# Alternating the order of the two row tiles from one matmul pair to the next

## Chip, cores and metric

The kernel runs on one core of one Trainium2 chip. The metric is the device time of that core in microseconds (us), the median of several executions. Ratios are computed as the mean time of one kernel's fast runs over the mean time of the other's fast runs of the same rounds, so they are not quite the ratio of the medians quoted beside them; a 95% interval stands with each. A single run of a kernel is marked as such.

## The reference

A causal convolution over time with 7 taps per head (weights by softmax), then a two-layer network with a Swish whose slope is learned:

```python
# x [8, 4096, 192], weight [8, 7], w_in [192, 2048], w_out [2048, 192], beta [2048]
w = softmax(weight, axis=-1)
conv[b, s, head, :] = sum_k w[head, k] * x_padded[b, s + k, head, :]   # 6 zeros of padding in front
t = conv.reshape(32768, 192)
h = t @ w_in
g = h * sigmoid(beta * h)
out = g @ w_out                                                       # [32768, 192] float32
```

The two matrix products are nearly all the arithmetic.

## The kernel before

The 192 channels are three groups of 64, and batches are handled in two halves (`h`). Rows 0-63 of SBUF hold one half, rows 64-127 the other. (SBUF tiles are what the matmuls read; PSUM tiles are what they write; TensorE does the matmuls, ScalarE the Swish, named `Silu` in the code, VectorE sums and copies.) So a matmul with a contraction of 64 uses only half of the rows of the array, and two of them, one on rows 0-63 (**tile A** below) and one on rows 64-127 (**tile B**), stream at the same time: the records below show them start 19 ns apart and go on for 82 or 216 ns. A *pair* is one matmul on each tile. The hidden layer uses the tiles for the two halves of the batch; the output layer uses them for the two halves of a 128-row contraction, whose partial sums VectorE adds afterwards. The two matmuls of a pair write different slices (`[:, 0]` and `[:, 1]`) of a PSUM tile.

```python
def hidden(s, fc):                     # one block of 128 hidden features, 2 x 512 tokens
    ...
    for j in range(NG):                # NG = 3 channel groups
        for h in range(2):
            rows = slice(h * DG, (h + 1) * DG)                    # 0-63, 64-127
            nc.tensor.matmul(ph[:, h, 0:n], w_in_s[rows, j, cols], cts[s][rows, j, 0:n],
                             start=(j == 0), stop=(j == NG - 1))  # 512 columns
    nc.scalar.activation(gs[s][:, fc, :, 0:n], ph[:, :, 0:n], AF.Silu, scale=beta[:, fc:fc+1])

def output(s, u):                      # 8 pairs: half of the 16 feature blocks of 128 tokens
    ...
    for i in range(u * per, (u + 1) * per):
        blk, fc = divmod(i, NF)
        ...
        for r in range(2):
            rows = slice(r * 64, (r + 1) * 64)
            nc.tensor.matmul(po[:, r, b * D : (b + 1) * D],
                             g[rows, fc, h, q * BLK : (q + 1) * BLK], w_out_s[rows, fc, :],
                             start=(fc == 0), stop=(fc == NF - 1))  # 192 columns
        ...                            # after fc 15: VectorE copies, adds, and a DMA stores

for s in range(N_ST + 1):              # N_ST = 33 steps, and a last pass with outputs alone
    for u in range(NF):                # 16 units a step
        if s < N_ST: hidden(s, u)
        if s > 0:    output(s - 1, u)
        ...                            # VectorE taps of a later convolution, DMA
```

A *period* is one unit: 3 hidden pairs and 8 output pairs, 22 matmuls. Each matmul has its own weight load, the instruction that puts its stationary operand into the array.

Of the kernel before, what the change touches and what calls it, by code (L numbers as in the profile page):

```python
# [17 lines left out]
def kernel(  # L18
# [335 lines left out]
    def hidden(s, fc):  # L354
        n = steps[s][2]
        if fc == 0:
            gs[s] = g_pool.tile([128, NF, 2, TOK], BF16, name="g")
        ph = psum_h.tile([128, 2, TOK], FP32, name="ph")
        cols = slice(fc * 128, (fc + 1) * 128)
        for j in range(NG):  # L360
            for h in range(2):
                rows = slice(h * DG, (h + 1) * DG)
                nc.tensor.matmul(  # L363
                    ph[:, h, 0:n],
                    w_in_s[rows, j, cols],
                    cts[s][rows, j, 0:n],
                    start=(j == 0),
                    stop=(j == NG - 1),
                )
        nc.scalar.activation(  # L370
            gs[s][:, fc, :, 0:n], ph[:, :, 0:n], AF.Silu, scale=beta[:, fc : fc + 1]
        )
# [3 lines left out]
    def store(s, h, q, n_q, osb):  # L376

        ch, t0, n = steps[s]
        p, c = divmod(ch, CHUNKS)
        if s < N_ST - 1:  # L380
            if q < n // BLK - 1:
                return
            n_q = n // BLK
        t = c * TOK + t0 + (q + 1 - n_q) * BLK
        nc.sync.dma_start(
            out=out_v[h, p, t : t + n_q * BLK, :].rearrange("(b q) d -> q b d", q=BLK),
            in_=osb[:, q + 1 - n_q : q + 1, :],
        )

    def output(s, u):  # L390

        g = gs[s]
        nb = steps[s][2] // BLK
        per = 2 * nb
        for i in range(u * per, (u + 1) * per):
            blk, fc = divmod(i, NF)
            h, q = divmod(blk, nb)
            b = q % 2

            single = s == N_ST - 1 and h == 1 and q >= nb - 2  # L400
            if single:
                b = 0
            if fc == 0 and b == 0:
                state["po"] = psum_o.tile([128, 2, TOK], FP32, name="po")
            if fc == 0 and q == 0:
                state["osb"] = osb_pool.tile([128, TOK // BLK, D], FP32, name="osb")
            po, osb = state["po"], state["osb"]
            for r in range(2):
                rows = slice(r * 64, (r + 1) * 64)
                nc.tensor.matmul(  # L410
                    po[:, r, b * D : (b + 1) * D],
                    g[rows, fc, h, q * BLK : (q + 1) * BLK],
                    w_out_s[rows, fc, :],
                    start=(fc == 0),
                    stop=(fc == NF - 1),
                )
            if fc == NF - 1 and (b == 1 or single):
                n_q = 1 if single else 2
                cols = slice((b + 1 - n_q) * D, (b + 1) * D)
                dst = osb[:, q + 1 - n_q : q + 1, :].rearrange("p b d -> p (b d)")  # L420
                if single:
                    nc.scalar.copy(dst, po[:, 0, cols])  # L422
                else:
                    nc.vector.tensor_copy(dst, po[:, 0, cols])  # L424
                nc.vector.tensor_tensor(dst, po[:, 1, cols], dst, ALU.add)  # L425
                store(s, h, q, n_q, osb)
# [19 lines left out]
    for s in range(N_ST + 1):  # L446
        if s + 2 < N_ST:
            queue.extend(conv_ops(s + 2))
        for u in range(NF):
            if s < N_ST:  # L450
                hidden(s, u)
            if s > 0:
                output(s - 1, u)
            if s == 0 and u in first_work:
                first_work[u]()
            n = pops.get(s, 24)
            pops_u = (u + 1) * n // NF - u * n // NF if s else u > 5
            for _ in range(pops_u):
                if queue:
                    queue.popleft()()  # L460
            if u == 0 and s + 4 < N_CH:
                cast(s + 4)
            if u == 1 and s + 2 < N_CH:
                xpose(s + 2)
# [30 lines left out]
```

## Time and profile before

| | before |
|---|---|
| time, median (first 3 runs) | 697.0 us (696.14 to 697.85) |
| TensorE busy in the profile | 99% |
| granted TensorE clock | 1.00 |
| one period in the steady part | 1.307 us |

From the page of the kernel before: busy time by engine (first line), and the chain of work that ended last, by engine and by line of the program (line 363 is the hidden matmul, line 410 the output matmul). PE is TensorE's matmuls, PEld its weight loads, DVE is VectorE, ACT is ScalarE, POOL is GpSimd. The granted clock is the share of its full speed that TensorE was allowed.

```profile
PE 686.9 (99%) x11465; PEld 525.9 (76%) x11465; DVE 553.2 (80%) x935; ACT 578.7 (83%) x545; POOL 69.8 (10%) x83
...
PE 96%; DVE 3%; ACT 0%; issue 0%
PE po L410 48%; PE ph L363 46%; DVE ct L346 2%; DVE ct L344 1%; PE ph L204 1%; PE ph L249 0%; PE po L236 0%; PE po L208 0%; DVE w_in_s L149 0%; ACT g L370 0%; PE po L249 0%; DVE xt L314 0%; DVE osb L425 0%; DVE ct L300 0%; DVE osb L424 0%
```

The costliest groups of the same page: count, busy time, mean duration of one, idle time before them and what ended it.

```profile
L370 ACT ACTIVATE g<-ph,beta 128x1024 bf16<-128x1024 f32 (+1 forms) x528 | 571.8, 1088 | 97.0 <-PE ph L363 93.1
L410 PEld LDWEIGHTS <-g 64*128 64x128 bf16 x8192 | 368.9, 94 | 102.4 <-issue 0.2
L410 PE MATMUL po<-w_out_s,g 64*128 64x192 bf16 x8192 | 429.8, 243 | 0.0
L363 PE MATMUL ph<-ct,w_in_s 64*128 64x512 bf16 (+1 forms) x3168 | 425.5, 370 | 2.8 <-ACT g L370 1.4
```

TensorE is the bound: it waits for ScalarE 1.4 us in all, while ScalarE waits for it 93.1 us. In the timeline of TensorE in the middle of the run (start, duration, engine, line, operation, count) one sees the period.

```profile
299.63 0.83 PE L363 MATMUL ph<-ct,w_in_s 64*128 64x512 bf16 x6
300.28 0.84 PE L410 MATMUL po<-w_out_s,g 64*128 64x192 bf16 x16
300.94 0.83 PE L363 MATMUL ph<-ct,w_in_s 64*128 64x512 bf16 x6
301.59 0.66 PE L410 MATMUL po<-w_out_s,g 64*128 64x192 bf16 x11
```

From 299.63 to 300.94 is one period. The durations of the two rows overlap: a record lasts 376 ns (512 columns) or 243 ns (192), but the same tile starts its next matmul 216 or 82 ns after the start. The ends of matmuls are modelled in this profile; the distance between starts is what counts. Single records of the trace give it (listed from the trace, times in us; `waits` and `signals` mark the matmul that waits for ScalarE to free PSUM and the one that tells ScalarE that the group is done):

```
before   start     after the one before it
output   201.486   63 ns
output   201.506   20 ns
hidden   201.569   63 ns     waits
hidden   201.588   19 ns
hidden   201.785  197 ns
hidden   201.804   19 ns
hidden   202.001  197 ns
hidden   202.020   19 ns     signals
```

Two starts 19 ns apart are one pair. The same tile starts again 63 + 19 = 82 ns later (192 columns; 82.4 on average) or 197 + 19 = 216 ns later (512 columns): 3 x 216 + 8 x 82.4 = 1307 ns, the whole period.

### The profile page before, as it was taken

How to read it: one execution, taken by the hardware profiler on the slowest of the kernel's cores; microseconds unless marked ns; L12 is line 12 of the kernel's file. 1: busy time of each engine (PE TensorE's matmuls, PEld its weight loads, DVE VectorE, ACT ScalarE, POOL GpSimd, SP SyncE). 2: the span in 40 equal slices, each digit the busy share in tenths (PEclk: the TensorE clock that was granted, in tenths of full speed). 3: DMA queues.
4: the chain of work that ended last, by engine and by line, in shares of the span. 5: the costliest groups of instructions: out<-in, count | busy, mean ns of one | idle time of the engine just before them, and what ended most of it. 6: DMA issues, size and time to landing. Idle time of an engine off the chain costs nothing.

```text
span 695.1 us, 24857 instructions
## 1 busy us (share of the span) xinstructions
PE 686.9 (99%) x11465; PEld 525.9 (76%) x11465; DVE 553.2 (80%) x935; ACT 578.7 (83%) x545; POOL 69.8 (10%) x83
## 2 busy tenths in 40 slices
PE   8899999999999999999999999999999999999997
PEld 6767777777777777777777777777777777777777
DVE  6999999998777987777987777987778987777222
ACT  5898888888888888888888888888888888888881
POOL 6934455000000000000000000000000000000000
PEclk9999999999999999999999999999999999999999
DMA  9999999922232022322023222032123122111012
GB/s 175 146 160 160 169 177 171 138 62 70 54 65 71 27 68 72 47 70 70 26 70 71 49 70 69 26 71 70 48 72 55 41 70 71 48 48 48 25 48 70
DMA packets 181497, 54.57 MB, mean 79 GB/s; under 512 B 146432, under 2 KB 181072, under 8 KB 181392
## 3 DMA queue, kind: packets, MB, share of 16 engines
q0 software_dynamic: 98048, 14.89, 29.9%
q1 hardware_dynamic: 83296, 38.09, 23.6%
q8 instruction: 89, 1.46, 0.9%
q14 instruction: 16, 0.13, 0.1%
q10 hardware_dynamic: 48, 0.01, 0.0%
HBM read 28.98 MB, written 37.29 MB: 95 GB/s over the span
## 4 chain that ended last, share of the span: by engine, by line
PE 96%; DVE 3%; ACT 0%; issue 0%
PE po L410 48%; PE ph L363 46%; DVE ct L346 2%; DVE ct L344 1%; PE ph L204 1%; PE ph L249 0%; PE po L236 0%; PE po L208 0%; DVE w_in_s L149 0%; ACT g L370 0%; PE po L249 0%; DVE xt L314 0%; DVE osb L425 0%; DVE ct L300 0%; DVE osb L424 0%
## 5 line engine op out<-in xcount | busy, mean ns | idle before, releaser
L370 ACT ACTIVATE g<-ph,beta 128x1024 bf16<-128x1024 f32 (+1 forms) x528 | 571.8, 1088 | 97.0 <-PE ph L363 93.1
L410 PEld LDWEIGHTS <-g 64*128 64x128 bf16 x8192 | 368.9, 94 | 102.4 <-issue 0.2
L410 PE MATMUL po<-w_out_s,g 64*128 64x192 bf16 x8192 | 429.8, 243 | 0.0
L363 PE MATMUL ph<-ct,w_in_s 64*128 64x512 bf16 (+1 forms) x3168 | 425.5, 370 | 2.8 <-ACT g L370 1.4
L346 DVE SCALAR_TENSOR_TENSOR ct<-xt,cw,ct 128x512 bf16<-128x512 bf16 x558 | 380.4, 746 | 0.0
L363 PEld LDWEIGHTS <-w_in_s 64*128 64x128 bf16 x3168 | 162.4, 94 | 56.9 <-issue 3.6
L424 DVE COPY osb<-po 128x384 f32<-128x384 f32 x127 | 70.8, 558 | 126.3 <-PE po L410 120.2
L425 DVE TENSOR_TENSOR osb<-po,osb 128x384 f32<-128x384 f32 x129 | 71.5, 554 | 6.0 <-ACT osb L422 1.6
L95 POOL DMA_DIRECT2D xd<-in_x_dram x60 | 54.3, 906 | 47.8 <-DMA xd<-in_x_dram 43.5
L344 DVE TENSOR_SCALAR ct<-xt,cw 128x512 bf16<-128x512 bf16 x93 | 31.6, 393 | 0.0
L422 ACT COPY osb<-po 128x192 f32<-128x192 f32 x2 | 0.6, 318 | 9.9 <-PE po L410 9.9
L320 POOL TENSOR_TENSOR w_out_s<-w_out_raw,beta_r 128x768 bf16<-128x768 f32 x4 | 5.9, 1500 | 2.3 <-DMA w_out_raw<-in_moe_w_out_dram 2.3
L204 PE MATMUL ph<-zeros 128*128 128x512 bf16 x8 | 3.8, 627 | 1.3 <-DVE warm L132 1.3
L249 PE MATMUL po<-xt_145,diag 128*128 128x256 f32 x28 | 4.4, 296 | 0.0
L249 PEld LDWEIGHTS po<-xt_145,diag 128*128 128x128 f32 x28 | 3.6, 189 | 0.7 <-issue 0.6
L149 DVE COPY w_in_s<-w_in_s 64x1536 bf16<-64x1536 bf16 x4 | 2.7, 699 | 1.5 <-DMA w_in_s<-in_moe_w_in_dram 1.4
L184 POOL DMA_DIRECT2D w_out_raw<-in_moe_w_out_dram x4 | 3.1, 782 | 0.0
L249 PEld LDWEIGHTS ph<-xt_145,diag 128*128 128x128 f32 x14 | 2.6, 269 | 0.7 <-ACT xt_145 L270 0.6
L249 PE MATMUL ph<-xt_145,diag 128*128 128x256 f32 x14 | 3.1, 375 | 0.0
L204 PEld LDWEIGHTS <-zeros 128*128 128x128 bf16 x8 | 0.9, 130 | 2.5 <-issue 1.3
L142 POOL DMA_DIRECT2D w_in_s<-in_moe_w_in_dram x4 | 2.6, 667 | 0.8 <-POOLq L479 0.8
L261 ACT CAST ct<-po 128x256 bf16<-128x256 f32 x1 | 0.4, 372 | 2.8 <-PE po L249 2.8
(46 smaller groups left out, 27.7 us busy)
## 6 DMA issues: line engine op xcount, KB each, us to landing
out_dram<-osb SPq DMA_DIRECT2D x60, 384.0 KB, 3.0
xd<-in_x_dram POOLq DMA_DIRECT2D x54, 198.0 KB, 14.6
w_out_raw<-in_moe_w_out_dram POOLq DMA_DIRECT2D x4, 384.0 KB, 9.6
out_dram<-osb SPq DMA_DIRECT2D x7, 192.0 KB, 3.8
xd<-in_x_dram POOLq DMA_DIRECT2D x6, 192.0 KB, 14.0
x_83<-in_x_dram SPq DMA_DIRECT2D x4, 192.0 KB, 3.9
w_in_s<-in_moe_w_in_dram POOLq DMA_DIRECT2D x4, 192.0 KB, 7.9
xt<-xd SPq DMA_TRANSPOSE x30, 4.6
```

The lines of the kernel that those rows point to most:

```text
L95: nc.gpsimd.dma_start(out=xd[r0:, :, h, :], in_=x_v[p, t0:t1, h, :].rearrange("t (c d) -> t c d", c=NG),)
L184: nc.gpsimd.dma_start(out=w_out_raw[:, c : c + 4, :], in_=w_out_v[:, c : c + 4, :])
L204: nc.tensor.matmul(pf[:, 0, :], zeros[:, 0:128], zeros, start=True, stop=True)
L249: nc.tensor.matmul(pv, diag[:, c, k, :], xt0[:, c, o : o + n], start=(k == 0), stop=(k == K - 1),)
L320: nc.gpsimd.tensor_tensor(w_out_s[:, c0 : c0 + n, :], w_out_raw[:, c0 : c0 + n, :], beta_r[:, c0 : c0 + n].unsqueeze(2).to_broadcast((128, ...
L344: nc.vector.tensor_scalar_mul(dst, src, scalar)
L346: nc.vector.scalar_tensor_tensor(out=dst, in0=src, scalar=scalar, in1=dst, op0=ALU.mult, op1=ALU.add)
L363: nc.tensor.matmul(ph[:, h, 0:n], w_in_s[rows, j, cols], cts[s][rows, j, 0:n], start=(j == 0), stop=(j == NG - 1),)
L370: nc.scalar.activation(gs[s][:, fc, :, 0:n], ph[:, :, 0:n], AF.Silu, scale=beta[:, fc : fc + 1])
L410: nc.tensor.matmul(po[:, r, b * D : (b + 1) * D], g[rows, fc, h, q * BLK : (q + 1) * BLK], w_out_s[rows, fc, :], start=(fc == 0), stop=(fc ...
L424: nc.vector.tensor_copy(dst, po[:, 0, cols])
L425: nc.vector.tensor_tensor(dst, po[:, 1, cols], dst, ALU.add)
```

## The change

The row tile that was issued last for one pair is issued first for the next: A B, B A, A B and so on. It joins two matmuls, and two weight loads, of the same tile in the program; presumably it was meant to let one tile be fed twice in a row, or to make the loads fall better. Nothing is added or removed.

```diff
         for j in range(NG):
-            for h in range(2):
+            for h in (0, 1) if (fc + j) % 2 == 0 else (1, 0):
                 rows = slice(h * DG, (h + 1) * DG)
                 nc.tensor.matmul(ph[:, h, 0:n], ...
...
-            for r in range(2):
+            for r in (0, 1) if fc % 2 == 0 else (1, 0):
                 rows = slice(r * 64, (r + 1) * 64)
                 nc.tensor.matmul(po[:, r, b * D : (b + 1) * D], ...
```

## The prediction

> **What bounds the kernel now.** TensorE. The page gives PE 99% busy; the chain of waits that ended last is 96% PE. The table by stretches shows PE busy 100.00 of 100 us from 100 to 600 us at a granted clock of 1.00, with DVE at 81 to 89 and ACT at 85. PE waits for ACT only 1.4 us in all: the others have slack.
>
> A timeline of a few microseconds in the middle repeats every 1.307 us: 3 hidden pairs of 512 columns and 8 output pairs of 192. The single records show why. A pair is one matmul on rows 0-63 (tile A) and one on rows 64-127 (tile B), streaming at the same time. The next matmul of the same tile starts 82.4 ns later (192 columns) or 216 ns later (512); 3 x 216 + 8 x 82.4 = 1307 ns, so the period is each tile's own streaming. At 2.4 GHz (the Trainium skill, "TensorE: Matmul & The Clock Gate", spec table) the columns alone take 3072 / 2.4 = 1280 ns: at most 2% could be gained. B starts 19 ns after A in the steady part and 3 ns after it near 25 us, with the same 82.4 ns pitch: A B A B hides the offset. Weight loads (94 ns each) begin 1.7 ns after the previous matmul of their own tile starts, also where no other tile stands between (the zero matmuls at the start), so they are prefetched.
>
> **What the change does.** No instruction is added or removed. Pairs become A B, B A, A B, ... In a period of 11 pairs, 10 boundaries now join two matmuls of the same tile; at the eleventh the parity repeats.
>
> **Cost.** The same page (Part 3, "The mechanism") says that matmuls start and end in program order and that only weight loads are pulled ahead, with about 4 ns between starts. This trace shows no matmul overtaking, and 2 to 4 ns as the smallest distance between the starts of two tiles. In B1 B2 A2, B2 waits until B1 has streamed, and A2, whose tile is free, waits behind B2, starting 2.5 to 3.3 ns after it. A3 starts a full stream after A2, and B3 again behind it. A pair takes stream + about 3 ns, and the 19 ns offset shrinks to about 3. Weight loads keep their lead of some 80 ns.
>
> Pairs after the start phase: 496 periods x 11, some 180 more in the first and last steps, about 5,600; 10/11 of them, 5,100, x 3 ns = 15 us, all on the critical path. Estimate: 697 + 15 = 712 us, range 703 to 724. Faster by over 2%: 2%. Within 2%: 46%. Slower: 52%.
>
> **What would show it.** Period 1.34 us instead of 1.307; starts within a pair 2 to 4 ns apart; same-tile starts 82.4 and 216 ns across a boundary; weight loads still 94 ns, starting just after a matmul of their tile; ACT's idle up by the same 30 ns per period; PE still 99% busy; clock still 1.00.
>
> **What would make it wrong.** If each tile had its own queue, A2 would start beside B1 and nothing changes (697). If two loads in a row for the same tile are not pulled ahead, 13 to 16 ns per pair are exposed (the offset that late loads left in this trace): 765 to 780 us. If handing over takes 2.5 ns rather than 3.3, the loss stays just below 2%.

## The result, and the profile after

The time did not move: 696.67 us median (696.32 to 697.35, 4 runs) against 696.57 us (4 runs, the first three with one more). The ratio is 1.0000 with an interval of 0.9983 to 1.0017. The predicted 712 us (703 to 724) did not come.

The same lines of the page of the changed kernel:

```profile
PE 686.8 (99%) x11465; PEld 529.2 (76%) x11465; DVE 551.7 (79%) x935; ACT 578.4 (83%) x545; POOL 70.9 (10%) x83
...
PE 97%; DVE 2%; ACT 0%; issue 0%
...
L370 ACT ACTIVATE g<-ph,beta 128x1024 bf16<-128x1024 f32 (+1 forms) x528 | 571.5, 1088 | 96.7 <-PE ph L363 92.5
L410 PEld LDWEIGHTS <-g 64*128 64x128 bf16 x8192 | 370.8, 94 | 100.3 <-DVE osb L425 0.2
L410 PE MATMUL po<-w_out_s,g 64*128 64x192 bf16 x8192 | 430.6, 243 | 0.0
L363 PE MATMUL ph<-ct,w_in_s 64*128 64x512 bf16 (+1 forms) x3168 | 426.4, 370 | 2.4 <-ACT g L370 1.6
```

And its timeline of TensorE in the middle:

```profile
299.78 0.84 PE L410 MATMUL po<-w_out_s,g 64*128 64x192 bf16 x16
300.44 0.83 PE L363 MATMUL ph<-ct,w_in_s 64*128 64x512 bf16 x6
301.09 0.84 PE L410 MATMUL po<-w_out_s,g 64*128 64x192 bf16 x16
301.75 0.61 PE L363 MATMUL ph<-ct,w_in_s 64*128 64x512 bf16 x4
```

From 299.78 to 301.09 is again 1.31 us. ScalarE's idle time before the Silu did not grow (92.5 us). At this grain the two profiles are the same. The single records hold the first clue:

```
after    start     after the one before it
hidden   202.380   62 ns
hidden   202.401   21 ns     waits
hidden   202.596  195 ns
hidden   202.617   21 ns
hidden   202.812  195 ns     signals
hidden   202.833   21 ns
```

In the program the matmul that waits is the first of its group and the one that signals is the last. Between 60 and 680 us the kernel before has 474 whole groups, and the records of all of them show the two in these places. In the changed kernel that holds for 236 of the 473 groups of that stretch, and in the other 237 the records look as above: the matmul that waits started *second* and the one that signals last but one. The starts no longer follow the program.

### The profile page after: what moved, and what is told of

It reads as the page before. It is cut to its first block, busy times and chain, and to the rows that moved or that the text cites. A ratio compares the mean times of both kernels' runs of the same rounds, so it can differ in the third digit from the quotient of the medians.

```text
span 694.6 us, 24857 instructions
## 1 busy us (share of the span) xinstructions
PE 686.8 (99%) x11465; PEld 529.2 (76%) x11465; DVE 551.7 (79%) x935; ACT 578.4 (83%) x545; POOL 70.9 (10%) x83
## 4 chain that ended last, share of the span: by engine, by line
PE 97%; DVE 2%; ACT 0%; issue 0%
PE po L410 48%; PE ph L363 47%; DVE ct L346 2%; PE po L249 1%; PE ph L204 1%; PE ph L249 0%; ACT g L370 0%; PE po L236 0%; PE po L208 0%; DVE ct L300 0%; DVE osb L425 0%; DVE osb L424 0%; ACT ct L261 0%; ACT osb L422 0%; DVE zeros L130 0%
## 5 line engine op out<-in xcount | busy, mean ns | idle before, releaser
L370 ACT ACTIVATE g<-ph,beta 128x1024 bf16<-128x1024 f32 (+1 forms) x528 | 571.5, 1088 | 96.7 <-PE ph L363 92.5
L363 PEld LDWEIGHTS <-w_in_s 64*128 64x128 bf16 x3168 | 164.2, 94 | 55.2 <-issue 3.3
L344 DVE TENSOR_SCALAR ct<-xt,cw 128x512 bf16<-128x512 bf16 x93 | 28.8, 363 | 0.0
```

Source lines behind the costliest of these rows:

```text
L344: nc.vector.tensor_scalar_mul(dst, src, scalar)
```

## The experiments

All give correct results. From e1 on, the matmuls of the two tiles stand on source lines of their own, so that the profile names the tile of each.

### e1: which tile starts when

The changed kernel, with the one matmul call of each loop split in two:

```diff
-                rows = slice(h * DG, (h + 1) * DG)
-                nc.tensor.matmul(ph[:, h, 0:n], w_in_s[rows, j, cols], ...)
+    def on_tile_a(j): nc.tensor.matmul(ph[:, 0, 0:n], w_in_s[0:64, j, cols], ...)      # line 361
+    def on_tile_b(j): nc.tensor.matmul(ph[:, 1, 0:n], w_in_s[64:128, j, cols], ...)    # line 364
+    ... the same for the output: tile A on line 394, tile B on line 397
```

> The changed kernel with the matmuls of rows 0-63 (tile A) and of rows 64-127 (tile B) on source lines of their own, so that the records name the tile. Theory 'own queue': each row tile takes its next matmul as soon as it has streamed the one before, so A and B starts do not follow the program; the same tile leads every pair by 20 to 21 ns although the program alternates, starts of one tile are 82 ns (output) and 216 ns (hidden) apart throughout. Theory 'elastic hand-over': starts keep the program's order, A B, B A, A B, so the leading tile alternates and the starts of one tile are alternately 62 and 103 ns apart. Both: about 697 us, period 1.307 us.

Measured: 696.11 us (one run; before 696.3). The timeline of TensorE, one output phase:

```profile
300.89 0.24 PE L394 MATMUL po<-w_out_s,g 64*128 64x192 bf16 x1
300.91 0.24 PE L397 MATMUL po<-w_out_s,g 64*128 64x192 bf16 x1
300.97 0.24 PE L394 MATMUL po<-w_out_s,g 64*128 64x192 bf16 x1
300.99 0.24 PE L397 MATMUL po<-w_out_s,g 64*128 64x192 bf16 x1
301.05 0.24 PE L394 MATMUL po<-w_out_s,g 64*128 64x192 bf16 x1
301.07 0.24 PE L397 MATMUL po<-w_out_s,g 64*128 64x192 bf16 x1
```

The program says L394, L397, L397, L394, L394, L397. The array started A, B, A, B, A, B. Between 60 and 680 us tile A leads every pair, by 18 to 20 ns, and the starts of one tile are 81 to 84 ns (output) and 215 to 217 ns (hidden) apart in the single records. The elastic hand-over, with 62 and 103 ns in turn, is refuted. Each tile takes its own next matmul when it has streamed the one before, although the program puts up to two of the other tile between.

### e2: how far a tile can run ahead

The kernel before, but with the 8 output pairs of a unit as eight matmuls on A, then eight on B:

```diff
-            for r in range(2):            # inside the loop over the 8 pairs
-                matmul(tile r, pair)
+        for r in range(2):
+            for pair in eight_pairs:
+                matmul(tile r, pair)
```

> The kernel before, but each unit's 8 output pairs are issued as 8 matmuls on tile A, then 8 on tile B. Strict program order of starts (what the prediction assumed): period 1.81 us, about 954 us. One matmul waiting per tile while others pass: 1.64 us, about 870 us. Two waiting per tile: about 786 us. Four: about 700 us. Tiles independent of each other over at least 8 matmuls: 1.307 us, 697 us, with A and B matmuls of the same eight running side by side in the records although the program puts them one after the other.

Measured: 716.02 us against 696.3; ratio 1.0274 (1.0251 to 1.0297). Strict order (954) and one or two waiting matmuls (870, 786) are refuted; it lies between the figures for two and for four. The timeline shows why (L361 and L364 hidden on A and B, L394 and L397 output on A and B):

```profile
300.06 0.41 PE L394 MATMUL po<-w_out_s,g 64*128 64x192 bf16 x3
300.24 0.25 PE L397 MATMUL po<-w_out_s,g 64*128 64x192 bf16 x1
300.31 0.24 PE L394 MATMUL po<-w_out_s,g 64*128 64x192 bf16 x1
300.33 0.24 PE L397 MATMUL po<-w_out_s,g 64*128 64x192 bf16 x1
300.39 0.24 PE L394 MATMUL po<-w_out_s,g 64*128 64x192 bf16 x1
300.41 0.24 PE L397 MATMUL po<-w_out_s,g 64*128 64x192 bf16 x1
300.48 0.24 PE L394 MATMUL po<-w_out_s,g 64*128 64x192 bf16 x1
300.49 0.32 PE L397 MATMUL po<-w_out_s,g 64*128 64x192 bf16 x2
300.58 0.39 PE L361 MATMUL ph<-ct,w_in_s 64*128 64x512 bf16 x1
```

The first matmul on B starts at 300.24, when A has just started its fifth (299.90 and 299.98 stand in a row above the cut, 300.06, 300.15 and 300.23 in the first row here) and three of A's eight are still pending (300.31, 300.39, 300.48). The program has all eight of A in front of it. In the single records B's first weight load starts at 300.232, 4 ns after A's fifth matmul; the matmul follows 4 ns later and is 10 ns longer than the others (253 against 243), with its load ending after the matmul's start: its weights came late. The same happens on the way back: the first hidden matmul on A (300.58) had to wait until only three of B's outputs were pending, 27 ns after A was free, and took 10 ns more. That is 37 ns a period; the records show a period of 1.345 us, 38 more than 1.307. All 461 periods between 60 and 680 us look like this: both first matmuls come 26 to 29 ns after their tile was free and 3 to 5 ns after their load started.

### e3: runs of three

The kernel before with the loops over `j` and `h` of the hidden matmuls exchanged: A A A B B B.

> The kernel before, but each group's three hidden matmuls on tile A come before its three on tile B. Strict program order of starts: period 1.67 us, about 880 us. One matmul waiting per tile: 1.37 us, about 727 us. Independent tiles: 697 us.

Measured: 697.42 us against 696.3; ratio 1.0015 (0.9999 to 1.0031). The tiles are independent over runs of three, without the 30 us of a single waiting matmul. The single records add one thing: B's first weight load of such a group started while all three hidden matmuls on A, 648 ns of streaming, were still pending. In e2 three pending matmuls were 247 ns. The reach is a count, not a time, nor a number of columns (1,536 here, 576 in e2).

### e4: runs of 8, 16 and 32 where nothing else runs

Only the last 11 us of the kernel before are changed, where the output matmuls of the last step are alone.

```diff
+        if last step: issue 32 pairs in runs of 8 per tile, 32 in runs of 16, 32 in one run of 32,
+                      16 in a run of 16, the rest alternating
```

> The kernel before, except in the last 11 us, where only output matmuls are left: the first 32 pairs are issued in runs of 8 per tile, the next 32 in runs of 16, the next 32 in one run of 32 per tile (64 matmuls and 64 weight loads), then 16 in a run of 16 and 16 alternating. If tiles are independent without a limit, every 32 pairs take 2.64 us (32 x 82.4 ns). If the window of pending instructions is finite, the stretch where the run exceeds it takes longer, up to 5.2 us; a limit of 64 instructions, weight loads counted, would let runs of 16 (32 instructions ahead) pass and hold runs of 32 up by a little at most. With strict order all three stretches take 4.6 to 5.2 us.

Measured: 700.49 us (one run; before 696.3). The run of 32 in the timeline:

```profile
686.43 2.31 PE L394 MATMUL po<-w_out_s,g 64*128 64x192 bf16 x26
688.50 0.25 PE L397 MATMUL po<-w_out_s,g 64*128 64x192 bf16 x1
688.58 0.24 PE L394 MATMUL po<-w_out_s,g 64*128 64x192 bf16 x1
688.60 0.24 PE L397 MATMUL po<-w_out_s,g 64*128 64x192 bf16 x1
688.66 0.24 PE L394 MATMUL po<-w_out_s,g 64*128 64x192 bf16 x1
688.68 0.24 PE L397 MATMUL po<-w_out_s,g 64*128 64x192 bf16 x1
688.74 0.24 PE L394 MATMUL po<-w_out_s,g 64*128 64x192 bf16 x1
688.76 2.31 PE L397 MATMUL po<-w_out_s,g 64*128 64x192 bf16 x26
```

A streams 26 matmuls with B idle, and again B starts (688.50) exactly when three of A are pending; then B streams 26 with A idle. The runs of 16 show the same with 10 in place of 26. The 32 pairs of this stretch took 4.66 us (A's first start at 686.17 to A's first of the next run at 690.83, rows outside the cut), against 2.64 for tiles free of each other. The limit is neither 64 instructions nor 32 matmuls but three matmuls of the other tile, whatever the length of the run.

### e5: the change by four

Output pairs as A A A A B B B B, B B B B A A A A; hidden pairs as before.

> The change at a coarser grain: the 8 output pairs of a unit as four matmuls on A, four on B, four on B, four on A, so runs of eight on one tile stand inside each unit; hidden pairs as before. Theory 'window': each tile runs on its own, but instructions enter in program order a window of about 8 pending ones (4 weight loads and 4 matmuls, as the runs of 8 to 32 showed: the other tile started when 3 matmuls of the run were still pending). Then a run of eight behind four of the other tile is just covered: about 697 to 702 us (a late weight load or two of 10 ns a period). Rival, a window of one matmul per tile: 1.48 to 1.65 us a period, 790 to 870 us. Rival, strict program order: over 870 us.

Measured: 715.1 us against 696.75; ratio 1.0263 (1.0248 to 1.0278). My expectation of 697 to 702 missed. The tiles again run on their own (the rivals said 790 and more), but a reach of eight instructions is too long. Counting in the records of e2 to e6, the other tile's weight load goes when five or six instructions stand in front of it, that is, it is itself the sixth or seventh; whether the load of the next matmul on the first tile, which starts 2 ns earlier, still counts can't be told. A replay of the program outside the chip gives an estimate. In it an instruction may start once at most six earlier ones have not started (a window of seven), a load starts 2 ns after the previous matmul of its tile or 4 ns after the matmul that lets it into the window, a matmul 4 ns after a late load, and a matmul with late weights takes 10.5 ns more. 1.344 us a period here, 1.344 for e2 and 1.655 for e6 (a window of six gives 2 to 4 ns more); a window of eight gives 1.307, 1.307 and 1.575. The records show 1.345, 1.345 and 1.657. In this kernel two switches a period land at the very end of the reach. At each, the tile starts 26 to 28 ns after it was free; along the chain that passes from tile to tile this is 8 ns of hand-over and 10 ns of late weights, some 18 ns a switch.

### e6: the change by whole groups

Hidden A A A B B B, outputs eight on B and eight on A, and the next unit mirrored: runs of 3, 11, 8 on alternating tiles.

> The change taken to whole groups: A A A B B B hidden, then eight on B and eight on A, the next unit mirrored, so runs of 3, 11, 8, 3, 11, 8 alternate between the tiles. Theory 'window of 8 instructions': the second tile of a run of 11 idles until 3 matmuls of the run are pending, so a period takes about 1.56 us, with the late weight loads 1.60: 825 to 850 us. If the limit were a time rather than a count, the other tile would start a fixed time before the end of a run: in a run that ends with hidden matmuls (216 ns each) fewer than three would be pending when it starts. Rival, no limit worth noting (window of 16 or more): 697 us. If the limit is set by something else in the runs of 8 (a wait for ScalarE or VectorE), the records will show a wait in place of pending matmuls.

Measured: 869.94 us against 696.75; ratio 1.2490 (1.2469 to 1.2511). Above the 825 to 850 expected, for the same reason as e5: the window is seven, not eight (1.656 us by the replay, 1.657 in the records). The timeline shows one tile alone again and again:

```profile
300.97 0.59 PE L364 MATMUL ph<-ct,w_in_s 64*128 64x512 bf16 x2
301.40 0.57 PE L397 MATMUL po<-w_out_s,g 64*128 64x192 bf16 x5
301.74 0.25 PE L394 MATMUL po<-w_out_s,g 64*128 64x192 bf16 x1
```

A's last hidden matmul started at 300.87 and had streamed 216 ns later, at 301.09. From then on B alone works off its last hidden and five output matmuls; A's first output starts at 301.74, again with three of B's pending (301.81, 301.90, 301.98 in the rows that follow). No wait for another engine holds it: in the records A's load and matmul carry no semaphore wait, and the load starts 4 ns after B's fifth output. The rival with a time as its limit is refuted by e3 rather than here, since no run of this kernel that is long enough ends with hidden matmuls.

The table by stretches of this kernel (the columns are the stretch, its length, and busy time with count of PE, PEld, DVE, ACT and POOL, then the clock, the DMA share and GB/s) is worth a look:

```profile
300.00:400.00 100.00, 100.00 (x1335) 78.08 (x1335) 66.32 (x114) 67.47 (x61) 0.00 (x0) 1.00 0.18 44
```

The same stretch of the kernel before:

```profile
300.00:400.00 100.00, 100.00 (x1688) 76.43 (x1684) 81.34 (x139) 85.12 (x78) 0.00 (x0) 1.00 0.25 58
```

Both say that PE was busy 100.00 of 100 us. The one is 25% slower: PE counts as busy when either tile is. Only the count of matmuls (1335 against 1688) tells that a tile idles about a fifth of the time.

### e7: the change by two

Output pairs as A A B B, B B A A: inside the outputs the longest run is four.

> The change with output pairs alternating by two: A A B B B B A A, so the longest run inside the outputs is four on one tile. Runs of 8 to 32 and alternation by four all showed the same reach: the first weight load of the other tile starts when three matmuls of the run are still pending, so a switch costs two times some 18 ns where the run just fills the reach. Here at each switch to the other tile at most three matmuls of the run are pending before the other tile's last one ends. Theory 'reach of three': 697 us, within 0.5%. If instead every switch after two or more costs 18 ns, there are about four a period: 697 + 512 x 37 to 74 ns = 716 to 735 us. Strict program order: about 710 to 730 us.

Measured: 696.45 us against 696.84; ratio 1.0000 (0.9983 to 1.0017). As the reach of three demands, and against the rival that every switch after two or more costs 18 ns (716 to 735).

### e8: a matmul that waits at the head

One hidden buffer in PSUM instead of two, the first hidden matmul on A put alone in front of the output pairs, these with B first, the other five hidden matmuls after them:

```diff
-    psum_h: bufs=2                        hidden(s, u); output(s - 1, u)
+    psum_h: bufs=1                        hidden: A, j = 0;  output(s - 1, u), B before A;  hidden: the rest
```

> A matmul on tile A that waits for ScalarE (only one hidden buffer in PSUM, so the first hidden matmul on A has to wait for the Silu each period), followed in the program by an output pair that begins on tile B and waits for nothing. If a tile's own queue holds its waiting matmul and lets the other tile pass, output matmuls of tile B start during the wait. If semaphore waits are served in program order ahead of the tiles, nothing of tile B starts until the waiting matmul does, then B starts within about 5 to 10 ns of it. Both: a longer period, since the Silu (1.11 us) is no longer hidden, roughly 2.4 to 2.6 us without passing, over 1200 us in all.

Measured: 1436.23 us (one run; the granted clock averaged 0.959 in it, but was 1.00 from 150 us on). The period was 2.69 us, above the 2.4 to 2.6 expected. The timeline from the end of one hidden group to the next wait (L361 hidden on A, L364 on B; L400 output on B, L397 on A):

```profile
302.87 1.11 ACT L371 ACTIVATE g<-ph,beta 128x1024 bf16<-128x1024 f32 x1 [1.63 <-PE ph L364]
304.04 0.37 PE L361 MATMUL ph<-ct,w_in_s 64*128 64x512 bf16 x1 [1.26 <-ACT g L371]
304.04 0.09 PEld L400 LDWEIGHTS <-g 64*128 64x128 bf16 x1 [1.56 <-issue]
304.04 0.09 PEld L397 LDWEIGHTS <-g 64*128 64x128 bf16 x1
304.04 0.34 PE L400 MATMUL po<-w_out_s,g 64*128 64x192 bf16 x2
```

And from the table of waits (total us, times, longest):

```profile
PEld L400 <- issue: 768.8, 512, 1.8
```

The matmul on A waited 1.26 us for the Silu. The weight load of B (L400) waited for nothing that the profile shows ("issue"), B was free, and still it started 2 ns after A's matmul. The records of all 512 groups show this: B's load 1 or 2 ns after A's waiting matmul, B's matmul 5 or 6 ns after it. So here a matmul that waits for a semaphore holds both tiles: the wait is served in program order, and only behind that point do the tiles go their own ways. What the holding costs was not measured, since no run has one buffer and the old order.

This also bears on the changed kernel, where in 237 groups a hidden matmul on A started before the one on B that carries the group's wait for the PSUM buffer. If an unmet wait holds both tiles, as here, A can only have passed one that was already met, so the buffer was free. That fits the correct results, but no run tests it by itself.

## Why the prediction was wrong, point by point

- **What bounds the kernel: right.** It is TensorE, by each tile's own streaming: 3 x 216 + 8 x 82.4 = 1307 ns. The changed kernel keeps exactly this sum.
- **Weight loads keep their lead: right.** They last 94 ns in both traces and start about 2 ns after the previous matmul of their tile.
- **"A2, whose tile is free, waits behind B2, starting 2.5 to 3.3 ns after it": this is the step that failed.** The prediction took it from the Trainium skill ("TensorE: Matmul & The Clock Gate", Part 3, "The mechanism": matmuls start and end in program order). In e1 A2 starts 82 ns after A1 and some 20 ns *before* B2, which stands in front of it. The term of about 3 ns a pair, 15 us in all, is nil.
- **"This trace shows no matmul overtaking": true, and worth nothing.** In the kernel before, the program's order A B A B and the order in which the tiles come free are the same, so nothing could overtake. The trace did hold a hint: A and B were 19 ns apart in the steady part and 3 ns near 25 us, at the same pitch of 82.4 ns. A constant but arbitrary offset fits two tiles that run freely; it was read as an offset that A B A B hides.
- **"The 19 ns offset shrinks to about 3": wrong with it.** It is 20 to 21 ns, with the same tile in front.
- **What would make it wrong: the first case named, that each tile has its own queue, is what the runs show**, within limits. The Trainium skill says this elsewhere ("TensorEngine Tiling (Array Packing)", "Tiling Modes", "Key Properties": tiles operate independently, and different tiles can execute weight loads and matmuls in parallel). Between two statements of the skill that pull apart, the prediction took the one that its trace could not test as the basis of its number.
- **Why the change could not gain either.** Both tiles already stream without gaps; each matmul takes about 2.5 ns beyond its columns at 2.4 GHz (1307 against an estimate of 1280 ns from the 2.4 GHz in the Trainium skill, "TensorE: Matmul & The Clock Gate", spec table; the trace agrees, 320 columns more take 133.6 ns more, 0.4175 ns each), and none of the orders tried took that away.

What stays open: whether the reach counts six or seven instructions, and whether it is a count of instructions or of matmuls, since every matmul here has one weight load.

## What to carry to other kernels

With two row tiles and one weight load for each matmul, as here, the order of the two tiles in the program is free as long as no tile's next matmul stands behind more than about three pending matmuls of the other: alternating by one or by two, and runs of three, cost nothing; by four costs 2.6%, eight in a row on each tile 2.7%, whole groups 25%. Other tilings were not run. So interleave the tiles finely, don't spend effort on which goes first, and don't put a matmul that waits for a semaphore in front of work of the other tile that could go. Check tile by tile, on source lines of their own: a busy share of 100% for TensorE is reached with one tile idle.

## What the Trainium skill lacked or had wrong

- "TensorE: Matmul & The Clock Gate", Part 3, "The mechanism", and Part 2, step 1, say that matmuls stay in program order, start and end. For matmuls on different row tiles the starts do not: in e1 each tile starts its own next one 82 ns after its last, against the program, and in 237 of 473 hidden groups of the changed kernel the matmul that waits for the buffer started second. The completion signal seems to stay in order: where the matmul that signals started 21 ns before the last one, ScalarE began 443 ns after the start of the signalling matmul, that is 422 ns after the last start; where the signalling matmul was the last itself, 413 ns after it (medians of 237 and 236 groups). The ends are modelled in the profile, so these runs do not test the order of ends.
- The same page gives a queue of 64 with a partial reorder window that pulls weight loads ahead. No run here shows a reach of that size between tiles: the other tile's first weight load went when three matmuls of the running tile were pending, in runs of 4, 8, 16 and 32 alike, that is as the sixth or seventh instruction. Its matmul came 4 ns after the load and took 10 ns more.
- No page says that a matmul waiting for a semaphore holds back the other tile: in e8 a wait of 1.26 us in the period shown, with B free and its load waiting for nothing, and in all 512 groups B's load 1 or 2 ns behind A's waiting matmul.
- "Perfetto Trace Analysis", "Identifying the Most-Contended Engine", warns that matmul busy time is a bad measure and offers MFU (the arithmetic done, as a share of the peak) and the summed time of the weight-load records over the window instead. Both do tell here: the matmuls in 100 us fall from 1688 to 1335, and the loads, 94 ns each, sum to 158.3 us in the kernel before and 125.3 us in e6. What the page lacks is that with two row tiles this sum passes 100% (158% when both tiles are fed), and that the busy time of `prof`, which counts overlapping records once, tells nothing: PE 100.00 in both, PEld 76.43 and 78.08. A busy record on either tile hides an idle one.
